# Rounding a weight's high part ahead of the add of its low word's bits

## The chip, the cores and the metric

The kernel runs on one core of a Trainium2 chip. The metric is the device time of one execution in microseconds; the kernel before takes 2156.36 us, the median of three runs (2156.23 to 2157.32). The core's engines work side by side, each through its own list of instructions in a fixed order, and wait for one another by semaphores: TensorE (PE, with its weight loads as PEld), VectorE (DVE), ScalarE (ACT), GpSimd (POOL) and SyncE (SP), which here issues nearly all transfers.

## The reference

Attention with normalized queries and keys comes first, for 8 batches of 448 tokens and 12 heads of 64. Its output x goes through a two-dimensional FFT of which the real part is kept, is added to x, normalized, and passed through a feed-forward block with two weight matrices:

```python
q_n, k_n = (rmsnorm(q, g_q), rmsnorm(k, g_k))
scores = scale * np.matmul(q_n, k_n.transpose(0, 1, 3, 2))
attn = softmax(scores);  x = attn @ v          # heads side by side: (8, 448, 768)
mixed = np.real(fft(fft(x, axis=1), axis=2))
u = x + mixed
un = (u - mean) / np.sqrt(var + 1e-06)
out = u + np.maximum(un @ w_ch1, 0.0) @ w_ch2  # w_ch1: 768 x 3072, w_ch2: 3072 x 768
```

The two weight matrices come as 64-bit floating-point numbers. The kernel turns each into two 32-bit numbers, a high part that TensorE's short fp32r format holds and the remainder, and multiplies in three passes (high by high, high by low, low by high).

## The kernel before, in words

The batches are pipelined. `aux(b)` is attention and FFT of batch b, `ffn(b, ...)` its feed-forward block; `merge` lets the code of `aux(b+1)` run beside that of `ffn(b)`. The tile framework's scheduler then lays each engine's list down once, by a timeline of its own; `behind` (L130) adds a bound for the conversions of the first stage, and `pace` (L905) one for the matrix products. So the order of the work around the change is not what the code says line by line, but what the scheduler makes of it.

The weights are cut into 60 pieces: 24 of w_ch1 (128x768 numbers, `up(m)`, 18 products each at L1019) and 36 of w_ch2 (128x512, `down(g, d)`, 12 products each at L1040). Batch 0 is the only one that converts. Thirteen pieces are converted early, beside the first attention (their tiles are called `mage`, `dble`, `w1e`, `w2e`; `convert_some`, L874). The other 47 are converted while batch 0's feed-forward block runs (`mag`, `dbl`, `w`). Each converted piece is also stored in DRAM (L820), and later batches load it from there (L832). The 64-bit words land in a tile `dbl` (tag X, two buffers), the bits are built in a tile `mag` (tag M, two buffers), and high and low part go to a tile `w` that belongs to one of two streams with three buffers each.

A conversion (`convert`, L765) has eight steps behind its load (L773, issued by SP):

- ACT: absolute value of the high words into `mag` (L776), and the low words scaled down in place in `dbl` (L777);
- DVE: clamp (L778), shift (L782), and merge of the top bits (L786), all in `mag`;
- POOL: add of the low word's bits to `mag` (L790), the last reader of `dbl`;
- ACT: high part, `mag` rounded into the first half of `w` (L791);
- DVE: low part, `mag` minus the high part, into the second half of `w` (L792).

Tags with few buffers set what waits: the load of the piece after next needs its `dbl` buffer free, so it waits for L790; L776 of the piece after next needs `mag` free, so it waits for L792; the high part needs a free `w` tile, so it waits until TensorE is through with the piece that had that tile three pieces back in its stream.

Other names: `un` is the normalized u and `unT` its transpose, `xr` and `xT` are attention outputs, `S`, `mn`, `P`, `sm` are scores, row minima, exponentials and their sums, `st` the sums for mean and variance, `smdf` the FFT's sum and difference, `h` and `o` the products' PSUM tiles, `hs` the hidden values, `acc` the block's accumulated output and `oT` its transpose, `qk` the transposed queries and keys, `ident` the identity for transposes, `rounded` low parts of the keys. Operations recorded by helpers all have line L115, so there the tile's name tells them apart.

Of the kernel before, what the change touches and what calls it, by code (L numbers as in the profile page):

```python
# [91 lines left out]
def spectral_block(ctx, tc, q, k, v, g_q, g_k, w1, w2, d1, d2, out, nb=B):  # L92
    nc = tc.nc
# [30 lines left out]
    def order(ins, before, kind, reason):  # L124
        tc.add_manual_dep(
            ins.ins, before.ins.name, mybir.DependencyInfo(kind, reason),
            reason="issue order",
        )

    def behind(ins):  # L130

        others = given.get(ins.ins.engine, [])
        if starting[0] and len(others) > LAG:
            order(
                ins, others[-1 - LAG],
                mybir.DependencyClass.NoSync, mybir.DependencyReason.DATA,
            )
# [23 lines left out]
    def wide(name, dtype=F32):  # L161
        return sb.tile([128, 1800], dtype, tag="X", name=name, bufs=2)
# [602 lines left out]
    def convert(src, bits, part, name):  # L765

        _, c, f = src.shape
        raw = wide(f"dbl{name}", U32)[:, : c * f].rearrange(  # L770
            "r (c f w) -> r c f w", c=c, w=2
        )
        nc.sync.dma_start(raw.rearrange("r c f w -> r c (f w)"), src)  # L773
        low, high = raw[:, :, :, 0], raw[:, :, :, 1]
        value = bits.bitcast(F32)
        behind(nc.scalar.activation(value, high.bitcast(F32), AF.Abs))  # L776
        behind(nc.scalar.activation(low, low, AF.Copy, scale=2.0**-29))  # L777
        behind(nc.vector.tensor_scalar(  # L778
            out=value, in0=value, scalar1=MIN_HIGH, scalar2=MAX_HIGH,
            op0=ALU.max, op1=ALU.min,  # L780
        ))
        behind(nc.vector.tensor_scalar(  # L782
            out=bits, in0=bits, scalar1=5, scalar2=2,
            op0=ALU.logical_shift_left, op1=ALU.logical_shift_right,
        ))
        behind(nc.vector.scalar_tensor_tensor(  # L786
            out=bits, in0=high, scalar=0xC0000000, in1=bits,
            op0=ALU.bitwise_and, op1=ALU.bitwise_or,
        ))
        behind(nc.gpsimd.tensor_tensor(out=bits, in0=bits, in1=low, op=ALU.add))  # L790
        behind(nc.scalar.copy(part[0], value))  # L791
        behind(nc.vector.tensor_tensor(  # L792
            out=part[1], in0=value, in1=part[0], op=ALU.subtract
        ))
# [3 lines left out]
    class Stream:  # L798
# [14 lines left out]
        def converted(self, p, name):  # L813
            hl = self.tile(p, name)
            n = hl.shape[2]
            bits = slot("M", f"mag{name}", U32)[:, : n * 128].rearrange(
                "r (c f) -> r c f", c=n
            )
            convert(piece_doubles(p), bits, [hl[:, k] for k in range(2)], name)
            nc.sync.dma_start(piece_kept(p), hl.bitcast(F32))  # L820
            return hl
# [317 lines left out]
```

## Time and profile before

| | |
|---|---|
| median of 3 runs | 2156.36 us |
| profiled execution | 2157.21 us, of which 2155.4 us span |
| TensorE busy | 2079.3 us (96%) |
| VectorE busy | 1544.9 us (72%) |
| ScalarE busy | 1028.5 us (48%) |
| GpSimd busy | 343.9 us (16%) |
| mean share of the 16 DMA engines | 0.57 to 200 us, 0.78 from 200 to 500 us, 0.63 after |

The profile is read by stages: the first attention and FFT until 182 us, batch 0's feed-forward block with the conversions from 182 to 471 us, and after that seven more blocks, in which nothing is converted. An engine's share over the whole span is a mean over these. A busy TensorE is not a TensorE at its peak, since products are pipelined; its idle time is what the steps below deal in.

### The profile page before, as it was taken

What the parts mean: (1) busy time and instruction counts of PE and PEld (TensorE: products, weight loads), DVE (VectorE), ACT (ScalarE), POOL (GpSimd) and SP (SyncE); (2) the same over time, 40 slices, a digit from 0 to 9 for tenths busy, and PEclk for the clock granted to TensorE, in tenths of its full rate; (3) what the DMA queues carried; (4) which work ended last, traced back from release to release, by engine and by line L of the source; (5) the groups of instructions that cost most, each with busy time, mean ns of one, the idle gap of its engine ahead of it and who ended that gap; (6) DMA issues with size and microseconds to landing.
All of it is one profiled execution on the core that took longest, in us unless ns stands there. A gap on an engine that the chain in (4) does not pass through costs nothing.

```text
span 2155.4 us, 31372 instructions
## 1 busy us (share of the span) xinstructions
PE 2079.3 (96%) x11256; PEld 1848.5 (86%) x11256; DVE 1544.9 (72%) x3002; ACT 1028.5 (48%) x2218; POOL 343.9 (16%) x200
## 2 busy tenths in 40 slices
PE   7877999999999999999999999999999999999998
PEld 4546777889999999999999999999999989999998
DVE  6787778887885788868787688857787578754122
ACT  6757876455552555335552455425553355422100
POOL 4324333321110111101110111101110011000000
PEclk8987999999999999999999999999999999999999
DMA  6547886687556855667566765558556674458874
GB/s 179 155 124 265 263 256 217 229 276 209 174 164 187 245 168 159 188 203 217 165 177 177 222 197 174 171 183 245 170 164 188 200 210 138 146 177 248 235 246 153
DMA packets 292913, 423.88 MB, mean 197 GB/s; under 512 B 181348, under 2 KB 219221, under 8 KB 292757
## 3 DMA queue, kind: packets, MB, share of 16 engines
q1 hardware_dynamic: 288322, 419.75, 64.1%
q10 hardware_dynamic: 4434, 2.11, 0.4%
q8 instruction: 90, 1.47, 0.3%
q14 instruction: 67, 0.54, 0.1%
HBM read 362.01 MB, written 65.31 MB: 198 GB/s over the span
## 4 chain that ended last, share of the span: by engine, by line
PE 79%; DVE 7%; DMA 6%; ACT 3%; issue 2%; POOL 2%; SPq 1%; POOLq 0%; DVEq 0%; ACTq 0%
PE o L1040 29%; PE h L1019 28%; PE S L407 5%; PE av L519 4%; PE pt L507 4%; DMA dbl<-w 3%; PE y L644 2%; POOL mag L790 1%; PE qk L343 1%; DVE mn L115 1%; DVE mag L786 1%; PE oT L976 1%; DMA u_dram<-u 1%; PE un L888 1%; DVE mag L778 1%
## 5 line engine op out<-in xcount | busy, mean ns | idle before, releaser
L1040 PE MATMUL o<-hs,w 128*128 128x448 f32 x3456 | 792.2, 372 | 4.9 <-DVE acc L115 3.2
L1019 PE MATMUL h<-unT,w 128*128 128x448 f32 x3456 | 783.0, 371 | 4.3 <-DVE hs L115 1.5
L1040 PEld LDWEIGHTS o<-hs,w 128*128 128x128 f32 x3456 | 637.7, 188 | 62.1 <-DVE acc L115 4.2
L1019 PEld LDWEIGHTS h<-unT,w 128*128 128x128 f32 x3456 | 640.0, 189 | 57.8 <-issue 2.2
L115 ACT ACTIVATE P<-S,mn 112x448 f32<-112x448 f32 x384 | 244.0, 638 | 222.5 <-DVE mn L115 208.7
L115 DVE TENSOR_REDUCE mn<-S 112x1 f32<-112x448 f32 x384 | 234.1, 617 | 43.3 <-PE S L407 34.1
L115 ACT ACTIVATE hs<-h 128x448 fp32r<-128x448 f32 x192 | 104.3, 543 | 277.9 <-PE h L1019 277.1
L115 DVE SCALAR_TENSOR_TENSOR hs<-h,hs 128x448 fp32r<-128x448 f32 x192 | 119.1, 620 | 129.8 <-ACT hs L115 128.4
L115 DVE TENSOR_TENSOR acc<-o,acc 128x448 f32<-128x448 f32 (+1 forms) x240 | 146.6, 613 | 87.9 <-PE o L1040 86.9
L115 POOL TENSOR_TENSOR qkn<-raw 112x1024 f32<-112x1024 f32 x36 | 69.4, 1927 | 686.4 <-PE qk L343 409.4
L115 POOL TENSOR_TENSOR ss<-ss,nhalf 112x16 f32<-112x16 f32 x48 | 142.0, 2959 | 203.8 <-DVE ss L115 195.1
L115 ACT CAST T<-pt 128x448 fp32r<-128x448 f32 x216 | 113.6, 533 | 124.7 <-PE pt L507 122.8
L115 DVE TENSOR_TENSOR T<-pt,T 128x448 fp32r<-128x448 f32 x216 | 132.3, 618 | 35.2 <-ACT T L115 34.1
L519 PE MATMUL av<-T,vhl 128*128 128x448 f32 x432 | 152.1, 384 | 0.0
L115 DVE TENSOR_SCALAR P<-P,sm 112x448 f32<-112x448 f32 x288 | 129.2, 487 | 4.6
L407 PE MATMUL S<-KD,QT 128*112 128x448 f32 x328 | 128.6, 392 | 2.2 <-ACT KD L115 1.9
L507 PE MATMUL pt<-ident,P 112*128 112x112 f32 x864 | 126.5, 258 | 0.0
L407 PE MATMUL S<-rounded,QT 128*112 128x448 f32 x328 | 120.4, 367 | 0.2 <-DVE rounded L115 0.2
L507 PEld LDWEIGHTS pt<-ident,P 112*128 112x128 f32 x864 | 104.3, 140 | 16.6
L790 POOL TENSOR_TENSOR mag<-mag,dbl 128x512 uint32<-128x512 uint32 (+1 forms) x47 | 78.8, 1677 | 159.3 <-DVE mag L786 131.2
L115 POOL TENSOR_TENSOR rstd<-st,nhalf 112x1 f32<-112x1 f32 (+2 forms) x32 | 19.6, 612 | 487.5 <-DVE st L115 480.5
L519 PEld LDWEIGHTS av<-T,vhl 128*128 128x128 f32 x432 | 80.9, 188 | 7.9
(120 smaller groups left out, 2499.5 us busy)
## 6 DMA issues: line engine op xcount, KB each, us to landing
w<-w SPq DMA_DIRECT2D x192, 768.0 KB, 4.5
w<-w SPq DMA_DIRECT2D x288, 512.0 KB, 3.9
dbl<-w SPq DMA_DIRECT2D x29, 512.0 KB, 4.8
dbl<-w SPq DMA_DIRECT2D x18, 768.0 KB, 4.9
raw<-q SPq DMA_DIRECT2D x96, 112.0 KB, 2.9
raw<-k SPq DMA_DIRECT2D x96, 112.0 KB, 5.0
values<-v SPq DMA_DIRECT2D x96, 96.0 KB, 4.4
u_dram<-u SPq DMA_DIRECT2D x24, 336.0 KB
```

The costliest lines, as they stand in the source:

```text
L115: ins = emit(*args, **kwargs)
L343: nc.tensor.transpose(pt[:, c * C : (c + 1) * C], qk[:, i, c].rearrange("t h d -> t (h d)"), ident[:C, :C],)
L407: ins = nc.tensor.matmul(s_, QT[:, h, cs], K[:, h], start=step == 0, stop=step == 1)
L507: nc.tensor.transpose(pt[:, c * C : (c + 1) * C], Pc[c][:, 512 * h + j * 128 : 512 * h + (j + 1) * 128], ident[:C, :C],)
L519: nc.tensor.matmul(av[:, :S], lv, T[:, i], start=(j == 0 and i == 0), stop=False)
L644: nc.tensor.matmul(o, src[:, par, t0 : t0 + n], D1[:, ri, par, cols], start=i != 1, stop=i != 0,)
L778: behind(nc.vector.tensor_scalar(out=value, in0=value, scalar1=MIN_HIGH, scalar2=MAX_HIGH, op0=ALU.max, op1=ALU.min,))
L786: behind(nc.vector.scalar_tensor_tensor(out=bits, in0=high, scalar=0xC0000000, in1=bits, op0=ALU.bitwise_and, op1=ALU.bitwise_or,))
L790: behind(nc.gpsimd.tensor_tensor(out=bits, in0=bits, in1=low, op=ALU.add))
L888: nc.tensor.transpose(pt[:, OFFS[i] : OFFS[i] + LENS[i]], uns[i][:, p * 128 : (p + 1) * 128], ident[: LENS[i], : LENS[i]],)
L1019: pace(nc.tensor.matmul(o, w[:, a, c], unT[c][:, z], start=n == 0, stop=n == 17))
L1040: pace(nc.tensor.matmul(o, w[:, a, f], hs[4 * g + f][:, z], start=n == 0, stop=n == 11))
```

## The change

Two lines of `convert` change places: the high part is rounded from `mag` before the low word's bits are added to it, not after. Since the add works in place, it now has to wait until ScalarE has read `mag`, and VectorE's subtraction, which needs the sum and the high part, waits for the add. The high part lacks the low word's bits; the low part takes them up, as it is the sum minus the high part.

```diff
         behind(nc.vector.scalar_tensor_tensor(
             out=bits, in0=high, scalar=0xC0000000, in1=bits,
             op0=ALU.bitwise_and, op1=ALU.bitwise_or,
         ))
+        behind(nc.scalar.copy(part[0], value))
         behind(nc.gpsimd.tensor_tensor(out=bits, in0=bits, in1=low, op=ALU.add))
-        behind(nc.scalar.copy(part[0], value))
         behind(nc.vector.tensor_tensor(
             out=part[1], in0=value, in1=part[0], op=ALU.subtract
         ))
```

In the changed kernel L790 is therefore ScalarE's copy and L791 GpSimd's add. The same instructions are issued, but the scheduler lays them down in another order on every engine, from the first conversion until some way into batch 1's block; from there to the end the lists are the same as before.

The first place is ScalarE's list at the end of batch 0's FFT, where the normalized rows `un_0` to `un_3` are made for the first feed-forward block. Before:

```order
L791 CAST w2e_1484<-mage_1485 128x768
L115 ACTIVATE un_2_1512<-u_2_1497,st_2_1498 111x768
L115 COPY xr_1_1529<-xT_290 128x672
L791 CAST w_0_0_1577<-mag_0_1578 128x768
L776 ACTIVATE mag_1_1591<-dbl_1_1592 128x768
L777 ACTIVATE dbl_1_1592<-dbl_1_1592 128x768
L115 ACTIVATE u_2_1497,st_2_1498<-un_2_1512 111x768
L776 ACTIVATE mag_2_1604<-dbl_2_1605 128x768
L777 ACTIVATE dbl_2_1605<-dbl_2_1605 128x768
L115 ACTIVATE un_1_1543<-u_1_1527,st_1_1528 112x768
```

And now, from the same conversion on (`w2e_1484` is the last of the early ones):

```order
L790 CAST w2e_1484<-mage_1485 128x768
L115 ACTIVATE u_0_1464,st_0_1465<-un_0_1482 113x768
L790 CAST w_0_0_1577<-mag_0_1578 128x768
L115 ACTIVATE un_2_1512<-u_2_1497,st_2_1498 111x768
L115 COPY xr_1_1529<-xT_290 128x672
L115 ACTIVATE u_2_1497,st_2_1498<-un_2_1512 111x768
L776 ACTIVATE mag_1_1591<-dbl_1_1592 128x768
L777 ACTIVATE dbl_1_1592<-dbl_1_1592 128x768
L115 ACTIVATE un_1_1543<-u_1_1527,st_1_1528 112x768
L790 CAST w_0_1_1590<-mag_1_1591 128x768
L115 ACTIVATE un_3_1559<-u_3_1545,st_3_1546 112x768
```

Both copies have moved up, ahead of `un_2`, and the two passes over `mag_2` and `dbl_2` that stood ahead of `un_1` now come behind `un_3`.

The second place is TensorE's list at the end of batch 0's block. `o_5_4` and `o_5_5` are the products of the last two pieces. Before:

```order
L1040 MATMUL o_5_4_4331<-hs_23_4251,w_0_5_4_4219 128x448 x3
L407 MATMUL S_0_1_0_4472<-KD_0_3425,QT_0_3424 112x448
L407 MATMUL S_0_1_0_4472<-rounded,QT_0_3424 112x448
L407 MATMUL S_0_1_1_4473<-KD_0_3425,QT_0_3424 112x448
L407 MATMUL S_0_1_1_4473<-rounded,QT_0_3424 112x448
L1040 MATMUL o_5_5_4347<-hs_20_3842,w_0_5_5_4254 128x448 x3
```

And now the last of the 22 rows' worth of other products that stand between the two, and the start of `o_5_5`:

```order
L976 MATMUL oT_0_1_4420<-ident,acc_1692 113x128
L976 MATMUL oT_1_0_4527<-ident,acc_1692 112x128 x3
L976 MATMUL oT_0_1_4420<-ident,acc_1692 113x128
L343 MATMUL qk_1_1_4630<-ident,qkn_1_4486 128x112 x4
L1040 MATMUL o_5_5_4347<-hs_20_3842,w_0_5_5_4254 128x448 x2
L976 MATMUL oT_1_1_4532<-ident,acc_1692 112x128 x2
L407 MATMUL S_1_0_0_4645<-KD_1_4564,QT_1_4563 112x448
L407 MATMUL S_1_0_0_4645<-rounded,QT_1_4563 112x448
L407 MATMUL S_1_0_1_4646<-KD_1_4564,QT_1_4563 112x448
L407 MATMUL S_1_0_1_4646<-rounded,QT_1_4563 112x448
L1040 MATMUL o_5_5_4347<-hs_20_3842,w_0_5_5_4254 128x448
L1040 MATMUL o_5_5_4347<-hs_21_4161,w_0_5_5_4254 128x448 x3
```

In all, 10 products of scores, 4+4 of `qk` and 3+1+3+1+2 of `oT` now stand between the end of `o_5_4` and the third product of `o_5_5`, the first that reads the piece's low part; before there were four.

The third place is VectorE's list for that last piece, `mag_5_5`. Before, between shift (L782) and subtraction (L792):

```order
L782 TENSOR_SCALAR mag_5_5_4255<-mag_5_5_4255 128x512
L115 SCALAR_TENSOR_TENSOR u_3_4177,st_3_4178<-x_110_4179,smdf_1_4117 112x384
L786 SCALAR_TENSOR_TENSOR mag_5_5_4255<-dbl_5_5_4256,mag_5_5_4255 128x512
L115 TENSOR_TENSOR acc_1692<-o_5_1_4283,acc_1692 128x448
L115 SCALAR_TENSOR_TENSOR u_3_4177,st_3_4178<-x_111_4184,smdf_1_4117 112x384
L115 TENSOR_SCALAR st_1_4121<-st_1_4121 112x1
L115 TENSOR_SCALAR st_3_4178<-st_3_4178 112x1
L115 TENSOR_TENSOR acc_1692<-o_5_2_4299,acc_1692 128x448
L792 TENSOR_TENSOR w_0_5_5_4254<-mag_5_5_4255,w_0_5_5_4254 128x512
```

And now, from the add of `o_5_4`'s result to the merge (L786):

```order
L115 TENSOR_TENSOR acc_1692<-o_5_4_4331,acc_1692 128x448
L115 TENSOR_SCALAR P_0_1_4469<-P_0_1_4469,sm_0_1_4471 112x448 x2
L115 TENSOR_REDUCE mn_0_2_4509<-S_0_2_1_4512 112x1
L782 TENSOR_SCALAR mag_5_5_4255<-mag_5_5_4255 128x512
L115 SCALAR_TENSOR_TENSOR ur_0_4412<-oT_0_0_4415,rstd_0_1562,ur_0_4412 113x384
L115 TENSOR_REDUCE mn_0_3_4575<-S_0_3_0_4577 112x1
L115 TENSOR_TENSOR QT_1_4563<-qk_1_0_4565,QT_1_4563 64x448 x2
L786 SCALAR_TENSOR_TENSOR mag_5_5_4255<-dbl_5_5_4256,mag_5_5_4255 128x512
```

and from there to the subtraction:

```order
L115 TENSOR_SCALAR sm_0_2_4510<-sm_0_2_4510 112x2
L115 TENSOR_REDUCE mn_0_3_4575<-S_0_3_1_4578 112x1
L115 SCALAR_TENSOR_TENSOR ur_1_4525<-oT_1_0_4527,rstd_1_1570,ur_1_4525 112x384
L115 RECIPROCAL sm_0_2_4510<-sm_0_2_4510 112x2
L115 SCALAR_TENSOR_TENSOR rounded<-qk_1_1_4630,gains,KD_1_4564 64x448
L115 TENSOR_SCALAR P_0_2_4508<-P_0_2_4508,sm_0_2_4510 112x448 x2
L115 TENSOR_SCALAR sm_0_3_4576<-sm_0_3_4576 112x2
L115 TENSOR_REDUCE ss_2_4780<-qkn_2_4778 112x16
L115 RECIPROCAL sm_0_3_4576<-sm_0_3_4576 112x2
L115 SCALAR_TENSOR_TENSOR rounded<-qk_1_1_4630,gains,KD_1_4564 64x448
L115 TENSOR_REDUCE mn_1_0_4643<-S_1_0_0_4645 112x1
L792 TENSOR_TENSOR w_0_5_5_4254<-mag_5_5_4255,w_0_5_5_4254 128x512
```

Before, the last piece's bits were shifted and merged around the adds of `o_5_0` and `o_5_1`; now its shift and its merge stand behind the add of `o_5_4`, and its subtraction behind a minimum over a score that stands in TensorE's list behind `o_5_5`'s first two products.

## Rows read from the trace of the kernel before

**Rows 1.** Stretches of the run, us: busy per engine (instructions), granted clock, DMA, GB/s
```profile
0.00:200.00 200.00, 148.05 (x707) 98.23 (x708) 155.61 (x275) 135.18 (x288) 70.54 (x49) 0.85 0.57 175
200.00:500.00 300.00, 284.33 (x1462) 241.52 (x1461) 242.44 (x430) 190.79 (x379) 100.47 (x61) 0.99 0.78 249
500.00:1800.00 1300.00, 1298.26 (x7248) 1188.11 (x7247) 986.93 (x1988) 618.20 (x1373) 163.54 (x84) 1.00 0.63 188
```

**Rows 2.** Conversion by line, 47 late pieces: ns min/median/max, first and last start
```profile
L786 DVE SCALAR_TENSOR_TENSOR mag<-dbl,mag x47: 674/692/971, 166.0 to 458.4; 128x512 uint32<-128x512 uint32 x29, 128x768 uint32<-128x768 uint32 x18
...
L791 ACT CAST w<-mag x47: 600/621/862, 170.1 to 461.2; 128x512 fp32r<-128x512 f32 x29, 128x768 fp32r<-128x768 f32 x18
```

**Rows 3.** SyncE's own waits, 140 to 500 us: total us, times, longest
```profile
SPq L773 <- POOL mag L790: 76.1, 42, 5.9
```

**Rows 4.** Waits of the engines, 140 to 500 us: total us, times, longest
```profile
ACT dbl L777 <- DMA dbl<-w: 25.4, 16, 4.2
ACT mag L776 <- DMA dbl<-w: 24.1, 11, 3.9
...
ACT w L791 <- POOL mag L790: 19.0, 14, 2.3
...
DVE w L792 <- ACT w L791: 8.3, 8, 1.8
```

**Rows 5.** Chain that ended last, one turn of a `dbl` buffer: start us, us, what
```profile
434.74 1.32 POOL mag L790
...
436.08 4.18 DMA dbl<-w
...
442.90 1.53 POOL mag L790
```

**Rows 6.** L792 alone, to the time given: VectorE busy us (instructions), as in rows 1
```profile
0.00:321.35 321.35, 29.94 (x37) 0.90 0.66 206
```

**Rows 7.** L1019 alone, to the time given: PE and PEld busy (instructions), as in rows 1
```profile
0.00:339.80 339.80, 56.40 (x235) 44.75 (x235) 0.91 0.66 205
```

**Rows 8.** Timeline, end of batch 0's block: start us, us, engine, line, operation, tiles
```profile
462.18 0.68 DVE L792 TENSOR_TENSOR w<-mag,w 128x512 fp32r<-128x512 f32 x1
...
468.56 2.62 PE L1040 MATMUL o<-hs,w 128*128 128x448 f32 x12
...
471.01 0.95 PE L888 MATMUL un<-ident,un 113*128 113x113 f32 x8
```

**Rows 9.** VectorE by line and tile, 455 to 475 us: count, busy us, mean ns, idle before
```profile
L115 DVE TENSOR_TENSOR acc<-o,acc 128x448 f32<-128x448 f32 x6 | 3.7, 612 | 1.3 <-PE o L1040 1.3
...
L115 DVE TENSOR_SCALAR P<-P,sm 112x448 f32<-112x448 f32 x4 | 1.6, 448 | 0.0
```

**Rows 10.** Timeline, end of batch 0's FFT, all engines: [idle before, what ended it]
```profile
163.40 1.83 POOL L790 TENSOR_TENSOR mage<-mage,dble 128x768 uint32<-128x768 uint32 x1 [19.69 <-ACT un L115]
...
163.57 2.08 DVE L782 TENSOR_SCALAR mag<-mag 128x768 uint32<-128x768 uint32 x1
...
167.13 1.84 POOL L790 TENSOR_TENSOR mag<-mag,dbl 128x768 uint32<-128x768 uint32 x1 [1.90 <-issue]
...
168.47 1.31 DVE L792 TENSOR_TENSOR w2e<-mage,w2e 128x768 fp32r<-128x768 f32 x1
168.58 0.94 ACT L115 ACTIVATE un<-u,st 111x768 f32<-111x768 f32 x1 [2.49 <-DVE st L115]
...
170.26 1.53 PE L676 MATMUL x<-ident,xr 128*112 128x128 f32 x6 [6.52 <-ACT xr L115]
...
176.27 0.92 ACT L115 ACTIVATE un<-u,st 112x768 f32<-112x768 f32 x1
...
182.01 0.74 PE L1019 MATMUL h<-unT,w 128*128 128x448 f32 x1 [1.36 <-ACT unT L115]
```

**Rows 11.** Timeline, an early conversion in the first attention, as in rows 10
```profile
122.84 0.84 ACT L791 CAST w2e<-mage 128x768 fp32r<-128x768 f32 x1 [1.75 <-POOL mage L790]
...
124.25 0.57 PE L450 MATMUL rt<-ident,rs 112*128 112x112 f32 x4 [0.95 <-ACT xT L115]
```

## The prediction

> **What bounds the kernel now.** I read the stretches first. From 500 us on TensorE is idle for 1.7 of 1300 us, so a time won or lost earlier reaches the end unchanged; until 200 us it is idle for 52 us, and from 200 to 500 us for 15.7 us, at a granted clock of 0.85 and 0.99 of full speed [rows 1]. The change lies in these two stretches, and what it does to TensorE's idle time there is the answer. Then the conversions by line: the copy takes 0.62 us for a 128x512 piece (29 of the 47 late ones) and up to 0.86 us for a 128x768 one (18) [rows 2]. Then the waits. SyncE holds the load of a piece back for GpSimd's add 42 times in 47, and ScalarE sits idle for the landing of `dbl` 16+11 times [rows 3, 4]: the two `dbl` buffers turn without rest, and a conversion can't start earlier than its buffer allows. One turn (add to add) is 442.90 - 434.74 = 8.2 us in the last stretch, half of it the transfer [rows 5]. TensorE's own list of waits has no wait for a weight piece, so the pieces come in time. How much in time: at 321.35 us the 37th subtraction has ended, the one of the 14th `up` piece (13 early pieces and 24 late ones) [rows 6], and that piece's first product is the 235th of L1019, just begun at 339.80 us [rows 7]: 18.5 us. The last piece is ready at 462.18 + 0.68 = 462.86 us and used at 468.56 us: 5.7 us [rows 8]. The cover is thin at the end alone.
>
> **The change part by part.** Removed: ScalarE's waits for the add, 19.0 us in 14 waits after 140 us [rows 4] and a few before. Added: GpSimd's wait for the copy, and VectorE's wait for the add. Instructions, sizes and transfers stay as they are. A piece's own chain is as long as before, merge, copy, add, subtraction instead of merge, add, copy, subtraction. What changes is that `dbl` is given back later, and the order of the lists.
>
> *The turn of the buffers.* Each turn gets the copy and one hand-over longer: 0.65 us for a small piece, 0.86 + 0.03 for a large one, on average (29 x 0.65 + 18 x 0.89) / 47 = 0.74 us. With 47 pieces through two buffers that is 23.5 x 0.74 = 17.4 us at the last piece if nothing absorbs it. In the middle, 31 pieces in, it is 11.5 us against 18.5 us of cover. The copy also needs a free `w` tile, so there the add, and with it the load behind it, now waits for TensorE as well; while the streams are full this costs cover, not time. VectorE's long FFT work between 370 and 395 us takes up part of the delay, because pieces wait for VectorE there in any case. From there 14 conversions, or 7 turns, are left: 7 x 0.74 = 5.2 us, against 5.7. By durations alone the last piece would just be in time.
>
> *The last piece in the new order.* But the scheduler has laid the lists down for a late last piece. Its shift and merge now stand behind the add of `o_5_4`, and its subtraction behind 11 more VectorE instructions, the last of which waits for a score that TensorE makes behind the first two products of `o_5_5`. From the end of `o_5_4`, on VectorE: `acc` 0.61, two scalings of `P` at 0.45, a minimum, `ur` and a second minimum at 0.61 each (as `acc`), the shift 0.43, two low parts of `QT` at 0.61, the merge 0.68; that is 5.7 us. Then to the end of the subtraction: two minima, `ur`, two `rounded` and the sum `ss` at 0.61, two `P` at 0.45, four small ones at 0.17, the subtraction 0.68; 5.9 us (`acc` and `P` from [rows 9], the merge from [rows 2], the subtraction from [rows 8]). Successive instructions of VectorE start about 0.08 us before the end of the one ahead, 21 times, so 11.6 - 1.7 = 9.9 us. In that time TensorE has ten score products and two of `o_5_5` at 2.62 / 12 = 0.22 us, and 18 transposes at 0.95 / 8 = 0.12 us at most, as listed with the change [rows 8]: 4.2 to 4.8 us. It would idle for 9.9 - 4.2 = 5.7 us where it did not idle before. From below: 0, if the real lists run so that something else of this chain had to be waited for anyway. From above: 17.4 - 5.7 = 11.7 us, the whole delay of the turns. I take 5.7, as it follows from waits that the lists fix.
>
> *The end of batch 0's FFT.* TensorE waits 6.5 us for `xr` and later for `un` here, and its first feed-forward product starts at 182.01 us [rows 10]. Two things move. The shift of `mag_0` took 2.08 us beside the add of 163.40 us; this add now starts a copy (0.86 us) later, when the shift is through. The merge of `mag_0` then falls under the add instead. The nearest row of a two-operand VectorE instruction under an add is the subtraction at 168.47 us: 1.31 us, ended 0.8 us after the add of 167.13 us had [rows 10]. Held like that, the merge ends near 167 us as before, and this part gives nothing. The order gives something: `un_2` starts when the copy behind that merge is through, at 167.9 instead of 168.58 us, and `xr` with it 0.7 us earlier; `un_1` no longer stands behind the passes over the third piece and can start when its own sums are there, near 173.5 instead of 176.27 us. Of these 2.8 us I carry 2.0 to the first product, since `un_3` comes behind one more copy. Between 0 (other waits take over) and 4.0 (the merge isn't held).
>
> The Trainium skill, SBUF — State Buffer, section Who interferes with whom, has a rule for these rows: a VectorE instruction with two inputs in SBUF takes its second one through the read interface that it shares with GpSimd, and whichever starts second is held until the other has ended. The subtraction's 1.31 us agrees; no merge in this trace shows it, since the longest of 47 is 0.97 us [rows 2]. By the rule the merge is held and the sum below stands; by the merge's own row it would be free, this part would give about 4 us, and the sum would be 2158.
>
> *The first attention.* At 122.84 us the copy of an early piece starts after 1.75 us of waiting for its add, a copy of attention's output stands behind it, and TensorE idles 0.95 us for that [rows 11]. The wait for the add is gone; I take 0.5 us of the 0.95 (0 to 1).
>
> *VectorE's wait for the add.* Its waits for the copy, 8.3 us in 8 [rows 4], become waits for the add. The new order puts the subtraction nearer to the merge: two instructions or fewer lie between for 10 of 60 pieces, against 4 before. Copy and add take 0.62 + 0.03 + 0.2 + 1.3 to 1.5 us, two VectorE instructions 1.2 us, so each such piece blocks VectorE for about 1.1 us: some 7 us more over 300 us, in which VectorE is busy for 242 [rows 1]. Queued behind it are the additions to `acc` and the low parts of `hs`, for which TensorE waits. I take 0.5 us (0 to 3).
>
> The sum, against the profiled execution's own 2157.21 us: +5.7 - 2.0 - 0.5 + 0.5 = +3.7, so 2160.9. That execution was 0.85 us above the median of the runs shown, so in terms of the median it is 2160.0 us, 0.17% more than 2156.36. What a measurement of this kernel can tell from no change is about 0.2%, 4.3 us.
>
> **The rivals.**
> *The turns bind (slower).* If the folds absorb nothing, the last pieces come 17.4 us later and TensorE waits 11.7 us in several places from about 400 us on; deciding is whether the delay at the last piece exceeds 5.7 us by more than the work that was pulled ahead. For it: 42 of 47 loads wait for the add. Against it: where VectorE is the one waited for, a late landing costs nothing. 2156.4 + 11.7 - 2.5 = 2165.6 us.
> *The front wins (faster).* The merge isn't held (4.0), attention gains its 1.0, and the last piece finds its gap filled. For it: the merge's row. Against it: the fixed order at the end. 2156.4 - 5.0 = 2151.4 us.
> *Nothing is left.* The gain in front meets a stall of 2 to 3 us at the end: 2156.4 us. For it: TensorE's list is full of other products there. Against it: these are only 4.2 us of work.
>
> **How the numbers follow.** The forecast, with a range of its own from 2157 to 2164, has 0.45; the binding turns 0.22, the front 0.15, nothing left 0.18. 2160.7 us is the border of slower: all of the turns and almost half of the forecast lie above it, 0.43. Below 2152.1 us lie most of the front's case and a little of the others, 0.17. Between them 0.40. The range goes from 2150 to 2171: from the front's time less 1 to the turns' time with 5 us more for what a new order adds.
>
> **What would show it.** In the changed profile: TensorE idle by about 5 us around the last piece's third product (L1040), between 465 and 485 us, waiting for `w` of L792; the first product of L1019 near 180 us; SyncE's waits for the add longer than 76.1 us; ScalarE without waits for GpSimd, VectorE with some 15 us of them. If TensorE waits for `w` from 400 us on, the turns bind; if the idle time until 200 us is well under 50 us, the front decides; if there is no idle time at the last piece, the step on the new order is wrong.

## The result, and the profile after

The changed kernel takes 2177.99 us (median of 5 runs, 2176.89 to 2184.42) against 2156.36 us before: 1.0104 times as long, 95% interval 1.0091 to 1.0118. That is 21.6 us more, above the end of the predicted range. The profiled execution took 2184.42 us, 6.4 us above that median; differences of the traces are larger than those of the medians by about as much.

The stretches, columns as in [rows 1]:

```profile
0.00:200.00 200.00, 154.62 (x724) 103.57 (x725) 156.70 (x277) 135.19 (x289) 68.63 (x49) 0.84 0.56 169
200.00:500.00 300.00, 265.51 (x1315) 220.81 (x1314) 244.43 (x412) 185.86 (x366) 103.56 (x61) 0.96 0.71 233
500.00:1800.00 1300.00, 1295.60 (x7222) 1185.47 (x7222) 973.94 (x1960) 606.40 (x1349) 160.81 (x82) 1.00 0.64 190
```

Until 200 us TensorE is idle for 45.4 us instead of 52. From 200 to 500 us it is idle for 34.5 us instead of 15.7 [rows 1], and its clock there is 0.96 instead of 0.99. So the front gained, and all that was lost, and more, was lost while the late pieces are converted. By milestones: the first feed-forward product of batch 0 starts 4.1 us earlier (177.9), the block takes 32.2 us longer (its end, where batch 1's first product starts, is at 500.15 instead of 472.05), the next one 3.2 us less, because 27 products and transposes have moved ahead of it, and the remaining blocks 2.4 us more. The sum is 27.3 us.

Of the 32.2 us, 18.8 are idle time of TensorE and 3.2 the products that moved in; of the rest, some 10 us, most is clock. Three stretches in which it runs near the lower of its two levels (1.2 and 2.4 GHz) stand out (columns as above, the clock is the third number from the right):

```profile
265.00:273.00 8.00, 5.97 (x21) 5.34 (x22) 7.76 (x10) 3.78 (x8) 4.30 (x2) 0.57 0.31 99
460.00:467.50 7.50, 6.92 (x23) 5.64 (x23) 6.10 (x15) 3.47 (x7) 3.06 (x3) 0.54 0.75 231
490.00:501.50 11.50, 9.21 (x23) 6.23 (x23) 10.38 (x25) 4.55 (x10) 4.53 (x2) 0.55 0.36 128
```

In each, TensorE had just been idle: for 3.6 us until 267.03, 2.0 us until 459.77, 3.2 us until 490.84. At 0.57, 0.54 and 0.55 of full speed over 8.0, 7.5 and 11.5 us, 12.1 us' worth of clock are missing; one shorter stretch and the one at the start of the block add 4.7 us, and the kernel before had 6.6 us of this in its own block. The difference is 10.2 us. Without what lies under idle time or behind the block it is 7.8 us, so that some 2 us of the 32.2 stay open. The length of a gap doesn't decide by itself: after gaps of 2.66, 2.78 and 2.44 us (until 342.04, 403.83 and 423.81 us) the clock stayed at its upper level.

What the conversions did, in the view of [rows 2] (ns min/median/max, first and last start):

```profile
L786 DVE SCALAR_TENSOR_TENSOR mag<-dbl,mag x47: 672/693/2579, 162.2 to 487.9; 128x512 uint32<-128x512 uint32 x29, 128x768 uint32<-128x768 uint32 x18
L790 ACT CAST w<-mag x47: 597/623/859, 164.6 to 490.2; 128x512 fp32r<-128x512 f32 x29, 128x768 fp32r<-128x768 f32 x18
L791 POOL TENSOR_TENSOR mag<-mag,dbl x47: 1292/1609/2802, 165.9 to 490.9; 128x512 uint32<-128x512 uint32 x29, 128x768 uint32<-128x768 uint32 x18
L792 DVE TENSOR_TENSOR w<-mag,w x47: 674/692/3143, 168.4 to 495.5; 128x512 fp32r<-128x512 f32 x29, 128x768 fp32r<-128x768 f32 x18
```

The add now starts 165.9 to 490.9 us, that is 325.0 us for 23 turns of a buffer, 14.1 us each; before it was 167.1 to 459.3, 12.7 us each. From the end of a merge to the start of its add, taken piece by piece from the trace, it was 0.30 us on average and is 1.81 us: 0.89 until the copy starts, 0.70 for the copy, 0.22 until the add starts. So `dbl` is held longer, from the first pass (L776) to the end of the add 8.2 us on average instead of 6.4; `mag`, held from the first pass to the subtraction, is not: 10.3 us instead of 10.5. The waits that answer to [rows 3, 4], from 140 to 500 us:

```profile
SPq L773 <- POOL mag L791: 112.2, 33, 8.4
```

```profile
POOL mag L791 <- ACT w L790: 98.0, 21, 9.1
```

```profile
ACT mag L776 <- DMA dbl<-w: 63.0, 32, 5.2
ACT w L790 <- DVE mag L786: 19.8, 17, 1.9
```

SyncE holds loads back for 112.2 us instead of 76.1, ScalarE waits for the landing in the first pass 32 times, and TensorE, which had no wait for a piece, now has some (140 to 520 us):

```profile
PE o L1040 <- ACT w L790: 3.2, 1, 3.2
PE o L1040 <- DVE w L792: 2.7, 2, 2.0
PE h L1019 <- DVE w L792: 1.3, 1, 1.3
```

These are 7.2 us, and TensorE is idle for 18.8 us more than before. For the larger part it waits for other results of ScalarE and VectorE, such as these:

```profile
PE S L407 <- ACT P L115: 4.7, 5, 1.6
PE o L1040 <- DVE hs L115: 4.1, 2, 3.6
```

The longest gap shows how that comes about. The piece of its product had been ready since 250.0 us. But ScalarE stood waiting for the landing of a later piece's `dbl`, with the first half of the hidden values `hs` behind it in its list, and VectorE needs that for the second half:

```profile
264.07 0.89 ACT L776 ACTIVATE mag<-dbl 128x768 f32<-128x768 f32 x1 [2.38 <-DMA dbl<-w]
265.78 0.54 ACT L115 ACTIVATE hs<-h 128x448 fp32r<-128x448 f32 x1
267.03 2.23 PE L1040 MATMUL o<-hs,w 128*128 128x448 f32 x5 [3.60 <-DVE hs L115]
```

The gaps until 403.83 us (2.78 us) and until 484.17 us (1.59 us) follow landings for which ScalarE waited 4.19 and 2.73 us in the same way. Such gaps were there before as well, but ScalarE's waits for landings have grown from 49.5 to 70.1 us. A buffer that comes late is thus paid for also where no piece is late. One gap is of another kind: ScalarE's copy waits for its merge (one of those held beside an add), and TensorE for what stands behind the copy in ScalarE's list:

```profile
340.57 0.83 ACT L790 CAST w<-mag 128x768 fp32r<-128x768 f32 x1 [1.89 <-DVE mag L786]
341.43 0.56 ACT L115 CAST KD<-KD 64x448 fp32r<-64x448 f32 x1
342.04 0.46 PE L407 MATMUL S<-KD,QT 128*112 128x448 f32 x1 [2.66 <-ACT KD L115]
```

Where the cover went shows at the first `up` piece behind VectorE's FFT work (the 18th). Its subtraction and its first product, before:

```profile
373.89 0.94 DVE L792 TENSOR_TENSOR w<-mag,w 128x768 fp32r<-128x768 f32 x1
...
389.03 1.27 PE L1019 MATMUL h<-unT,w 128*128 128x448 f32 x5
```

and after:

```profile
386.64 0.95 DVE L792 TENSOR_TENSOR w<-mag,w 128x768 fp32r<-128x768 f32 x1
389.70 0.98 PE L1019 MATMUL h<-unT,w 128*128 128x448 f32 x4
```

There were 389.03 - 374.83 = 14.2 us of cover, and there are 2.1. From here on the cover is thin, and four of the last 16 pieces come late: the next one by 1.9 us, the last by 5.4. The last piece, whose load the chain of waits shows issued when the add two pieces back is through, and slow to land:

```profile
472.27 1.62 POOL mag L791
473.90 8.31 DMA dbl<-w
482.29 0.66 ACT mag L776
```

and the rest of it in the timeline, which answers to [rows 8]:

```profile
487.91 2.23 DVE L786 SCALAR_TENSOR_TENSOR mag<-dbl,mag 128x512 uint32<-128x512 uint32 x1
490.17 0.62 ACT L790 CAST w<-mag 128x512 fp32r<-128x512 f32 x1 [1.89 <-DVE mag L786]
490.84 0.94 PE L1040 MATMUL o<-hs,w 128*128 128x448 f32 x2 [3.23 <-ACT w L790]
490.92 1.29 POOL L791 TENSOR_TENSOR mag<-mag,dbl 128x512 uint32<-128x512 uint32 x1 [1.33 <-issue]
495.50 0.69 DVE L792 TENSOR_TENSOR w<-mag,w 128x512 fp32r<-128x512 f32 x1
496.25 4.10 PE L1040 MATMUL o<-hs,w 128*128 128x448 f32 x10 [0.67 <-DVE w L792]
```

The end of batch 0's FFT, which answers to [rows 10]:

```profile
161.87 1.83 POOL L791 TENSOR_TENSOR mage<-mage,dble 128x768 uint32<-128x768 uint32 x1 [20.53 <-ACT w2e L790]
162.20 2.31 DVE L786 SCALAR_TENSOR_TENSOR mag<-dbl,mag 128x768 uint32<-128x768 uint32 x1
...
165.86 1.85 POOL L791 TENSOR_TENSOR mag<-mag,dbl 128x768 uint32<-128x768 uint32 x1 [2.17 <-issue]
165.99 2.53 DVE L792 TENSOR_TENSOR w2e<-mage,w2e 128x768 fp32r<-128x768 f32 x1
...
177.94 0.74 PE L1019 MATMUL h<-unT,w 128*128 128x448 f32 x1 [1.87 <-ACT unT L115]
```

The merge under an add is held for 2.31 us, as forecast, but it ends at 164.51 us and not near 167, since all of this runs earlier than before.

### The profile page after: what moved, and what is told of

The parts are those of the page before. It is cut to its first block, busy times and chain, and to the rows that moved or that the text cites. A ratio compares the mean times of both kernels' runs of the same rounds, so it can differ in the third digit from the quotient of the medians.

```text
span 2182.6 us, 31344 instructions
## 1 busy us (share of the span) xinstructions
PE 2091.3 (96%) x11256; PEld 1855.6 (85%) x11256; DVE 1556.7 (71%) x3002; ACT 1027.6 (47%) x2218; POOL 345.1 (16%) x200
## 4 chain that ended last, share of the span: by engine, by line
PE 72%; DMA 5%; DVE 2%; issue 1%; ACT 1%; SPq 0%; POOL 0%; DVEq 0%; ACTq 0%; POOLq 0%
PE o L1040 27%; PE h L1019 26%; PE S L407 5%; PE av L519 4%; PE pt L507 4%; DMA ur<-u_dram 2%; PE y L644 1%; DMA dbl<-w 1%; PE qk L343 1%; DMA u_dram<-u 1%; DMA u_dram<-ur 1%; PE av L524 1%; PE x L676 1%; PE oT L976 1%; PE ab L721 1%
## 5 line engine op out<-in xcount | busy, mean ns | idle before, releaser
L1019 PE MATMUL h<-unT,w 128*128 128x448 f32 x3456 | 782.0, 371 | 5.2 <-DVE hs L115 2.0
L1019 PEld LDWEIGHTS h<-unT,w 128*128 128x128 f32 x3456 | 639.6, 189 | 59.9 <-DVE hs L115 2.4
L407 PE MATMUL S<-KD,QT 128*112 128x448 f32 x328 | 129.2, 394 | 10.2 <-ACT P L115 4.7
L791 POOL TENSOR_TENSOR mag<-mag,dbl 128x512 uint32<-128x512 uint32 (+1 forms) x47 | 78.0, 1661 | 158.9 <-ACT w L790 98.0
```

What stands on the lines that cost most here:

```text
L407: ins = nc.tensor.matmul(s_, QT[:, h, cs], K[:, h], start=step == 0, stop=step == 1)
L1019: pace(nc.tensor.matmul(o, w[:, a, c], unT[c][:, z], start=n == 0, stop=n == 17))
```

## The experiments

Theory 1 is that the turns of the two `dbl` buffers bind: what stands between merge and add is paid in each turn, uses up the cover, and then TensorE waits. Theory 2 is that the new lists block VectorE and ScalarE, which work in order. Each ratio is to runs of the kernel before on the same chip, with its 95% interval.

**Three `dbl` buffers.** In the changed kernel, and as a control in the kernel before:

```diff
-        return sb.tile([128, 1800], dtype, tag="X", name=name, bufs=2)
+        return sb.tile([128, 1800], dtype, tag="X", name=name, bufs=3)
```

> The changed kernel with three `dbl` buffers instead of two; its data flow is the same. Theory 1 (the turns of the two `dbl` buffers bind: the copy now lies inside a turn, merge's end to add's start went from 0.30 to 1.81 us on average over the 47 late pieces): a third buffer takes the turn away, the last piece is ready by about 465 us as before, and the time comes back by 15 us or more, to 2155 to 2163 us. Theory 2 (the new lists block engines that work in order, VectorE behind the subtraction that waits for the add, ScalarE behind the copy that waits for the merge): the buffers don't matter and the time stays at 2172 to 2180 us, with VectorE's waits for the add above 10 us.

> The kernel before with three `dbl` buffers, the control of the run above. If the turns also held the kernel before back, it gains 2 us or more; TensorE had no wait for a piece there, so both theories expect 2153 to 2158 us, within 0.2% of before.

Measured: 2168.64 us (1.0061, 1.0046 to 1.0076) for the changed kernel, 2158.25 us (1.0005, 0.9996 to 1.0014) for the control. Every late piece has 7.5 us of cover or more, so half of the loss goes with the turns; 10 us between the two remain, and neither theory had said half. ScalarE now waits for the other tile with two buffers:

```profile
ACT mag L776 <- DVE w L792: 32.6, 24, 3.1
```

**The sum in a tile of its own.** The copy stays ahead of the add, but the add needn't wait for it:

```diff
+        total = sb.tile([128, 900], U32, tag="sum", name=f"sum{name}", bufs=2)[
+            :, : c * f // 2
+        ].rearrange("r (c f) -> r c f", c=c)
         behind(nc.scalar.copy(part[0], value))
-        behind(nc.gpsimd.tensor_tensor(out=bits, in0=bits, in1=low, op=ALU.add))
+        behind(nc.gpsimd.tensor_tensor(out=total, in0=bits, in1=low, op=ALU.add))
         behind(nc.vector.tensor_tensor(
-            out=part[1], in0=value, in1=part[0], op=ALU.subtract
+            out=part[1], in0=total.bitcast(F32), in1=part[0], op=ALU.subtract
```

> Copy ahead of the add as in the changed kernel, but the add writes its sum into a tile of its own (two buffers), so it needn't wait for the copy, and `mag` is free after copy and add. Theory 1: the turn is as short as before (merge to add 0.3 us), so the time falls back to 2150 to 2160 us. Theory 2: the subtraction still waits for the add and the copy still stands ahead in ScalarE's list, so most of the loss stays, 2168 to 2180 us. A third theory, that VectorE loses by adds that now lie beside its two-input instructions (L786 and L792 took 89.6 us instead of 74.9), would show as a sum of both near 85 us or more whatever the time.

Measured: 2155.44 us (0.9998, 0.9988 to 1.0009). Merge to add is 0.22 us, and the whole loss is gone, with the copy first and the subtraction still behind copy and add. What costs is that the add waits for the copy. (The tile also lets `mag` go earlier, so this alone doesn't name the buffer; but the changed kernel held `mag` no longer than the one before.) The two-input instructions took 38.6 + 44.7 = 83.3 us, near the third theory's 85, without any loss: that theory falls.

**Early pieces only.** `first` chooses the place of the copy, here and in the next three:

```diff
+        first = name[0] == "e"
+        if first:
+            behind(nc.scalar.copy(part[0], value))
         behind(nc.gpsimd.tensor_tensor(out=bits, in0=bits, in1=low, op=ALU.add))
-        behind(nc.scalar.copy(part[0], value))
+        if not first:
+            behind(nc.scalar.copy(part[0], value))
```

> The copy goes ahead of the add in the 13 early pieces alone; the 47 late ones are as before. Both theories put the loss into the late pieces: 2150 to 2158 us. If the gain at the end of the FFT (first feed-forward product at 177.9 instead of 182.0 us) comes from the early pieces, the time is 2152 us with that product near 178 us; if it comes from the order of the first late ones, 2156 us with the product near 182 us.

Measured: 2156.80 us (1.0004, 0.9988 to 1.0019), in ten runs from 2149.33 to 2162.74. The loss is in the late pieces. In the profiled run, the fastest of the ten, the first feed-forward product starts at 175.7 us; the median shows no gain, so the front's 4 us are there in traces but aren't shown as time.

**Head and tail.** `first` is `name[0] == "e" or PIECES.index(...) < 41`, and then `name[0] == "_" and PIECES.index(...) >= 41`:

> The copy goes ahead of the add in the 13 early pieces and in the first 31 late ones; the last 16 late pieces are as before. Theory 1 (a delay adds up, turn by turn, until the cover of about 8 us that VectorE's FFT work leaves to the last 16 pieces is used up): the first 31 pieces have 10 to 20 us of cover and pay nothing; 2154 to 2160 us. Theory 2 (each conversion blocks engines that work in order, for itself): the loss goes by the number of pieces, 31 of 47, and the time is 2168 to 2174 us.

> The reverse: only the last 16 late pieces (from the 18th `up` piece on) have the copy ahead of the add. Theory 1: 8 turns, each longer by 1.5 us, are 12 us against 8 us of cover at the end, and the delays of the first 31 are missing: 2159 to 2170 us. Theory 2: 16 of 47 pieces' worth of the loss, 2161 to 2166 us. With the run above: by theory 1 the losses of head and tail add up to much less than the whole 21 us, by theory 2 to the whole.

Measured: 2166.99 us for the head (1.0049, 1.0034 to 1.0064), 2163.97 us for the tail (1.0036, 1.0023 to 1.0049). The losses, 11.1 and 8.1 us, add up to 19.2, nearly the whole. That is what theory 2 had said of the sum, and my expectation from theory 1 for the head was wrong, though the head's loss lies below theory 2's range too. The trace of the head says why in part. Its 18th `up` piece:

```profile
384.98 0.95 DVE L796 TENSOR_TENSOR w<-mag,w 128x768 fp32r<-128x768 f32 x1
388.38 0.57 PE L1023 MATMUL h<-unT,w 128*128 128x448 f32 x2
```

The head hands over 2.4 us of cover instead of 14.2, and conversions of the old form don't rebuild it: the last piece is late by 2.0 us. The first 31 pieces aren't late, but they pay with cover that the last 16 need. Late pieces are the smaller part here, though: TensorE waits for them for 1.4 us in the head and not at all in the tail, where the thinnest cover is 0.8 us. The rest of these two losses is waits for other results, and clock.

**The last piece as before** (`first = name != "_0_5_5"`):

> The changed kernel with the last piece alone converted as before. The prediction's theory (the loss is the last piece in its new order): 2166 to 2172 us. Theory 1: the last piece is late because its buffer comes free late, so nothing but its own copy is gained: 2174 to 2180 us.

Measured: 2179.35 us (1.0103, 1.0086 to 1.0121). Nothing is gained, so the loss doesn't come from that piece's own copy and add. The lists around it are still those of a late piece, though (its merge starts at 490.45 us, its subtraction at 498.04); what these lists cost by themselves isn't separated here.

**A longer turn in the old order.** The kernel before, with this ahead of its add (`spare` as `total` above):

```diff
+        behind(nc.gpsimd.tensor_tensor(out=spare, in0=bits, in1=low, op=ALU.add))
```

> The kernel before, with a second add on GpSimd ahead of the add, into a spare tile that nobody reads: copy and add keep their old order, ScalarE and VectorE get no new wait, but `dbl` is given back 1.3 to 1.9 us later in each turn, about as much as the copy and its wait cost in the changed kernel (1.5 us). Theory 1: the same loss, 2170 to 2182 us, with pieces late from the 18th `up` piece on. Theory 2: no new wait ahead of a copy or a subtraction, so 2155 to 2162 us.

Measured: 2195.45 us (1.0183, 1.0168 to 1.0198), 39.5 us more, beyond what theory 1 said. The spare add:

```profile
L793 POOL TENSOR_TENSOR sum<-mag,dbl x47: 1279/1637/2666, 169.9 to 507.9; 128x512 uint32<-128x512 uint32 x29, 128x768 uint32<-128x768 uint32 x18
```

Merge to the real add became 2.19 us and a turn 14.7 us; pieces are late from the 19th `up` piece on, with the copy behind the add as ever. So a longer hold brings this kind of loss without the new order. (It isn't the hold of `dbl` alone: the copy waits for its add for 29.0 us in 17 waits instead of 19.0 in 14 [rows 4], GpSimd has 82 us more work, and some of that stands beside VectorE's. These aren't separated here. TensorE's waits for a piece are 3.9 us.)

**Three `dbl` and three `mag` buffers.** As in the first pair, and `"M": 3` in the table of slots:

> The changed kernel with three `dbl` and three `mag` buffers. With three `dbl` buffers alone no piece was late any more (cover of 7 us or more), but the time stayed 11 us above before, and ScalarE waited 32.6 us in 24 waits for `mag`, which is held from the first pass to the subtraction. Theory 1, extended (the turns of `mag` took the place of those of `dbl`): the rest goes too, 2154 to 2161 us. Theory 2 (VectorE's and ScalarE's waits for add and merge, in the order of their lists): it stays, 2165 to 2171 us, with VectorE's waits for the add still near 17 us.

> The kernel before with three `dbl` and three `mag` buffers, the control of the run above. It has cover everywhere, so both theories expect no change, 2153 to 2160 us.

Measured: 2164.73 us (1.0039, 1.0026 to 1.0052) for the changed form, 2167.27 us (1.0040, 1.0023 to 1.0057) for the old one. The control's expectation was wrong: more buffers cost the old form 11 us too. But between equal buffers the change costs nothing any more, though VectorE still waits for the add:

```profile
DVE w L792 <- POOL mag L791: 10.0, 10, 2.0
```

Against its control, then, theory 2's waits cost nothing here, as far as two kernels with different lists can be compared; the time alone is nearer theory 2's range than theory 1's. The control's data flow is that of before, so I put its loss down to the order that its lists got: its first feed-forward product starts at 187.3 us instead of 182.0, and its next block takes 255 us instead of 249, with TensorE waiting for batch 1's `un` at its end (columns of the timeline):

```profile
722.41 1.30 PE L888 MATMUL un<-ident,un 113*128 113x113 f32 x6 [1.99 <-DVE u L115]
724.51 1.01 PE L888 MATMUL un<-ident,un 112*128 112x112 f32 x4 [0.80 <-ACT un L115]
```

The changed kernel with three `dbl` buffers alone has the same two waits, and the same 255 us:

```profile
724.13 0.99 PE L888 MATMUL un<-ident,un 113*128 113x113 f32 x6 [1.45 <-DVE u L115]
726.24 0.60 PE L888 MATMUL un<-ident,un 112*128 112x112 f32 x4 [1.11 <-ACT un L115]
```

Its remaining 10 us are thus at least in part such an order, found by the old form as well.

**The copy on GpSimd.**

```diff
-        behind(nc.scalar.copy(part[0], value))
+        behind(nc.gpsimd.tensor_copy(part[0], value))
```

> The changed kernel with the copy on GpSimd instead of ScalarE, ahead of the add in the same list: the turn gets the copy's own duration there and no wait for another engine, and ScalarE is rid of 60 copies and of every wait for a merge in front of them. Theory 1: the loss follows from merge's end to add's start; if the copy takes 0.7 to 1.5 us there, that is 0.9 to 1.7 us against 1.81 in the changed kernel, and the time is 2164 to 2178 us. Theory 2: the blocked lists of ScalarE are gone, 2154 to 2162 us.

Measured: 2184.55 us (1.0131, 1.0116 to 1.0147), 6.6 us above theory 1's range and far from theory 2's. Merge to add is 2.10 us, more than I had worked out: the copy starts 0.26 us behind the merge and takes 0.85, but the add starts 0.99 us behind the copy, since GpSimd's other work, copies of other pieces included, often stands between. The copy itself and the longest of TensorE's waits:

```profile
L790 POOL CAST w<-mag x47: 604/822/1925, 161.7 to 496.1; 128x512 fp32r<-128x512 f32 x29, 128x768 fp32r<-128x768 f32 x18
```

```profile
PE o L1040 <- DVE w L792: 13.4, 6, 5.0
```

ScalarE has no part in this turn, and the loss is larger than with it. Here late pieces make much of it: some 20 of the 47 come late.

**The sum apart, and three `dbl` buffers.**

> The sum in a tile of its own (where the loss was gone) and three `dbl` buffers besides: copy and add run side by side, and no turn binds. This would beat both kernels if any of the 15.7 us that TensorE idles in batch 0's block before came from late pieces. Theory 1: none did, since TensorE had no wait for a piece there, so 2152 to 2159 us. A gain of 5 us or more would speak for pieces that were late in a way the waits don't show.

Measured: 2163.39 us (1.0034, 1.0021 to 1.0047). That is above what I had expected. No kernel beat both; this one is slower than with two buffers, though its last piece has 12 us of cover, and its first feed-forward product starts as late as 187.7 us.

With two buffers, merge to add and the loss go together:

| kernel | merge to add, mean us | against before, us |
|---|---|---|
| sum apart | 0.22 | -1.6 (no change within its interval) |
| before | 0.30 | 0 |
| early pieces only | 0.30 | -0.3 (no change within its interval) |
| tail | 0.89 | +8.1 |
| head | 1.34 | +11.1 |
| changed | 1.81 | +21.6 |
| last piece as before | 1.94 | +23.4 |
| copy on GpSimd | 2.10 | +28.5 |
| longer turn | 2.19 | +39.5 |

The loss goes with the buffers' turn, in all nine kernels, and with the add's wait for the copy it is gone. How the longer turn reaches TensorE is shown in part: through late pieces, through engines that wait in their lists for a late landing, and through the clock behind the gaps. How much of the 21.6 us is each of these, and how much the order that the scheduler made around them, stays open: each kernel gets its own lists, and the three-buffer kernels show that an order by itself can be worth 7 to 11 us.

## Why the prediction was wrong

**The step that failed is "the turn of the buffers".** It put 0.74 us into each turn, the copy and one hand-over, and let TensorE's and VectorE's other work absorb it, so that the last piece would "just be in time". The turn got 1.51 us: the copy doesn't start when the merge ends, it waits 0.89 us for its engine, and the hand-over to the add is 0.22 and not 0.03. The trace held that wait: before, the copy started 1.80 us after its add's end on average, which cost nothing as it lay outside the turn. I took the copy's duration and not its start. The step also looked for the price at the pieces alone, and waits for pieces are 7.2 of the 18.8 us by which TensorE's idle time grew; the others came through the lists of ScalarE and VectorE.

**The cover was added up wrongly too.** In the middle, 31 pieces in, the piece itself came 5.4 us later, where the step had 11.5; but the add that frees its buffer came 12.8 us later, so the buffers were as late as the step said. That VectorE's long FFT work "takes up part of the delay" was the reverse of what happened then. That work began at 369.4 us before and at 369.0 after. The 18th `up` piece's merge, 5 us ahead of it before (it ended at 364.3), fell behind its start and ended at 379.8; the piece came 12.8 us later, and its cover fell from 14.2 to 2.1 us. From there the delay grew by 8.2 us more over 14 pieces, 1.2 us per turn, where the step had 0.74, and by 12.4 us at the last piece alone.

**The last piece in the new order (+5.7)** is there as waits: 3.23 us at `o_5_5`'s first product, 0.67 at its third. From its first pass to the end of its subtraction the piece takes 13.9 us instead of 8.75. So the step found a real stall, but a small part of the loss: the piece's load had already come late (landed at 482.2 us), and with that piece converted as before the time is 2179.35 us. By that the late list looks like an effect of the delay and not its cause, but no run takes the list away by itself. (In the step's working, the 11 instructions ahead of the subtraction are 12, as its sum counts them; and by the rows that it names TensorE's work there is 4.8 us and the stall 5.1: the 4.2 that it used has no row.)

**The rival "the turns bind"**, given 0.22, named the right mechanism as far as the runs go. Its price of 11.7 us was 0.74 us times 23.5 less the cover; with 1.51 it would have been 35.5 - 5.7 = 29.8 us, against 21.6 measured. Its statement that "where VectorE is the one waited for, a late landing costs nothing" fell with the FFT work.

**What no term had** is the clock. Idle time was priced as itself; some 8 of the 32.2 us in block 0 were products at the lower level behind it.

**The end of the FFT (-2.0)** had the right sign and half the size: -4.1 us in the profile, with the merge held as forecast; as time no gain is shown. The **attention (-0.5)** was right in kind: that copy no longer waits, and TensorE's 0.95 us idle [rows 11] is gone. **VectorE's waits for the add** were forecast at some 15 us and are 12.3 in 11 waits; they cost nothing that the runs show.

The rule of the Trainium skill weighed in the prediction (SBUF — State Buffer, section Who interferes with whom) is borne out on the merge, where no row of before showed it: no merge took longer than 0.97 us there [rows 2], and beside adds that now come at other times merges take up to 2.58 us. Not every instruction of GpSimd holds them: five merges of the kernel before lie within its `ss` instructions (112x16, 2.9 to 3.2 us long) and took 0.68 to 0.96 us.

## What to carry to other kernels

When a step is moved inside the time in which a buffer is held, its price is its own duration, the wait for its engine and both hand-overs, times the turns of the buffer; the wait is invisible before, as it costs nothing there. Compare this with the cover of every late consumer behind the last long stretch of other work, not with cover in the middle, and look for items that stand just ahead of such a stretch: one that slips behind its start falls back at once. Cover isn't the whole account either: look up what stands in an engine's list behind the instruction that waits for the next load, since a late buffer holds that up too, with every piece in time. If the step must come first, give the later one an output of its own, so that it needn't wait: that brought all of the time back here.

## What the runs showed that I had not expected

- VectorE's two-input instructions, 0.67 to 0.97 us alone, were held up to 2.58 us (merge) and 3.14 us (subtraction) beside GpSimd; in sum the 47 merges went from 37.0 to 46.4 us and the subtractions from 37.9 to 43.2.
- GpSimd's copy to fp32r, where nothing stretched it, took 0.61 us for a 128x512 and 0.82 us for a 128x768 piece, ScalarE's 0.62 and 0.83; the engine was no slower there, only busier.
- More buffers made the kernel before slower: +1.2 us with three `dbl` (no change within its interval), +11.2 us with three `dbl` and three `mag`.
